# Five blocks of up to 512 tokens in both feed forwards of a sparse-attention and two-feed-forward kernel, with a new order of all the work around them

## The chip, the cores and the metric

The kernel runs on one core of a Trainium2 chip. Its time is the device time of one execution in microseconds (us), the median over several runs. A profile of one execution shows five engines that work in parallel, each in the order of its own queue: PE (TensorE: matmuls, with PEld for its weight loads), DVE (VectorE), ACT (ScalarE), POOL (GpSimd) and SP, which here only issues transfers.

## What is computed

Cut to what matters (4 sequences of 576 tokens, 8 heads of 64, so 2304 tokens of 512):

```python
# heads 0-3: local mask, 0 <= i - j < 32; heads 4-7: strided mask, i >= j and i % 32 == j % 32
scores = where(mask, q @ k.T / sqrt(64), -1e9)
x = softmax(scores) @ v                     # 2304 x 512, all heads side by side
h = x @ w_in                                # 512 x 2048, first feed forward ("moe")
x = (h * cos(h)) @ w_out                    # 2048 x 512
h = x @ w_in2                               # second feed forward ("moe2")
P = a0 + a1*h + a2*h**2 + a3*h**3
Q = 1 + |b0|*|h| + |b1|*h**2
out = (P / (Q + 1e-6)) @ w_out2
```

The weights arrive as 64-bit words of float64 (read as pairs of int32) and are decoded on the chip. Each fp32 product of the feed forwards is made of three matmuls: high part times high part, high times low, low times high.

## The kernel before

**Attention** is done in 32 items: `n` is a half sequence of 288 tokens (0 to 7), `pr` one of four pairs of heads. An item is scores (`att_s`, PE), maximum and subtraction or a softmax with a bias (DVE, POOL, ACT), exponentials (ACT), row sums and their reciprocals (DVE), the scaling (`att_norm`, POOL), transposes (`att_t`, PE) and their copies (`att_te`, ACT), the product with v (`att_o`, PE), and the split of the result into a high part `xh` (ACT) and a low part `xl` (DVE) in `att_oe`.

**A feed forward** goes over blocks of tokens, and in each block over 16 slices `f` of the 2048 inner columns. One block and one `f` is a step `g`. A step has 12 matmuls of the first layer (`l1`, line 415) into a bank `h`, elementwise work on `h`, and 12 (first feed forward) or 3 for every 128 tokens (second) matmuls of the second layer (`l2`, line 434), which are issued `LAG` steps later. In the first feed forward the elementwise work is called by letters: U (phase as an integer, ACT; `u` on DVE), K (a copy of `h`, ACT), V (fraction, DVE), N (sine, ACT), M (times `h`, DVE), G (high part `gh`, ACT), H (low part `gl`, POOL; `h` on DVE). Before, the blocks of the first feed forward have 256, 256, 352 and five times 288 tokens, the two of 256 sharing one set of four banks `y`; the second has six blocks of 384.

**Weights** of the first feed forward (32 tiles of 128 x 512) are decoded while the first steps run: two ACT instructions per tile (`dec_abs`), two on DVE (`dec_ops`, lines 156 and 158), then a high part on ACT and a low part on POOL or DVE (`w_split`). Those of the second are decoded later with three DVE instructions per tile, written to memory and read back.

**What sets the order.** Nothing is reordered by a scheduler: instructions are issued as the program writes them (`manual_schedule`). Before step 0 stands the list `START` of hand-written commands; from step 0 on, the string `ORD[g]` (or `C_ORD`) gives the order of a step's letters on ACT, DVE and POOL, and tables of step numbers (`TAB1`, `TAB2`, `TABE`, `TABO`, `W2ABS`, `DSTEP`) say in which step attention items, loads and decodes go. Before, `START` holds the whole of half `n` = 0 and the scores of half `n` = 1; the transposes and products of `n` = 1 come in steps 0 to 6. PSUM has eight banks: two `a`, two `h`, four `y`.

Of the kernel before, what the change touches and what calls it, by code (L numbers as in the profile page):

```python
# [8 lines left out]
F32 = mybir.dt.float32  # L9
# [10 lines left out]
NT = B * S  # L20
# [14 lines left out]
NB2 = 384  # L35
LAG = 3
LAG_AB = 2
RING = 3 * HS
HALF_COL = [0, HS, 2 * HS, 0, HS, 0, HS, 0]
NEG = -1e30  # L40
ABUFS = 4
BLAG = 7
NWARM = 38
NKEEP = 25
W2TAB = [(-7, -4, -3, -2, -1), (0, 3, 4, 4, 4), (4, 7, 8, 8, 9)]
TAB = ((-4, -2, -1, 0, 6, 9, 11), (-3, -1, 0, 1, 6, 10, 12), (0, 12, 2, 3, 6, 11, 13), (1, 13, 4, 5, 6, 12, 14))
# [12 lines left out]
ORD = {}
for _g in (0, 1, 23):  # L60
    ORD[_g] = "ukjVTswxyzNMabpqGHL"
COPY = {ord(c): None for c in "Kk"}
NPRE = 4
EVB, STB = 4, 6
LATE_OE = False
DSTEP = [0, 1, 2, 3, 4, 5, 6, 8, 10, 12, 14, 16]
# [11 lines left out]
W2ABS = [[25, 28, 29, 30, 31], [34, 37, 38, 38, 38], [37, 40, 41, 41, 42], [41, 44, 45, 45, 46], [48, 51, 52, 52, 52], [52, 55, 56, 56, 57], [57, 60, 61, 62, 63], [64, 67, 68, 68, 68], [68, 71, 72, 72, 73], [73, 76, 77, 78, 79], [80, 83, 84, 84, 84], [84, 87, 88, 88, 89], [89, 92, 93, 94, 95], [96, 99, 100, 100, 100], [100, 103, 104, 104, 105], [105, 108, 109, 110, 111]]  # L80
BLAG = 8
START = ['cst ACT', 'lq 0 0', 'lq 0 2 ACT', 'load 2 0', 'lv 0 1', 'lv 0 3 w0', 'lq 0 3', 'lq 0 1 ACT', 'load 0 0', 'lv 0 0', 'load 0 1', 'load 1 0 ACT', 'load 1 1', 'warm 38', 'lv 0 2 w0', 'masks', 's 0 0 y', 's 0 1 y', 's 0 2 y', 's 0 3 y', 'lq 1 0', 'ab', 'lq 1 2', 'lq 1 1', 'load 2 1', 'load 3 0', 'load 3 1', 'red 0 0', 'lv 1 0', 'exps 0 0', 'lq 1 3', 'ms 0 1', 'ex 0 1', 'red 0 2', 'lv 1 1', 'exps 0 2', 'norm 0 0 POOL', 'ms 0 3', 'ex 0 3', 'load 4 1', 'sum 0 1', 'norm 0 2 POOL', 'norm 0 1 POOL', 'sum 0 3', 'warm 29', 'abs 0 0', 'abs 0 1', 't 0 0 h', 'load 4 0', 'te 0 0', 'd 0 0 0', 'norm 0 3 POOL', 'o 0 0', 'd 0 1 0', 'd 0 0 1', 'd 0 1 1', 'd 0 0 2', 'd 0 1 2', 't 0 1 y', 'abs 1 1', 'te 0 1', 'oe 0 0', 'split 0 1 POOL', 'abs 1 0', 't 0 2 h', 'o 0 1', 'd 1 1 0', 'd 1 1 1', 'd 1 0 0', 'te 0 2', 'load 6 1', 'd 1 0 1', 'split 0 0 POOL', 'd 1 0 2', 't 0 3 y', 'oe 0 1', 's 1 0 y', 'te 0 3', 'd 1 1 2', 'o 0 2', 'split 1 0 POOL', 'oe 0 2', 'split 1 1 POOL', 'o 0 3', 's 1 1 y', 'abs 2 0', 'abs 2 1', 'd 2 0 0', 'd 2 1 0', 'abs 3 0', 'd 2 0 1', 'd 2 1 1', 'abs 3 1', 's 1 2 y', 's 1 3 a', 'red 1 0', 'd 2 1 2', 'red 1 1', 'd 2 0 2', 'exps 1 0', 'oe 0 3', 'split 2 0 POOL', 'exps 1 1', 'red 1 2', 'split 2 1 POOL', 'd 3 1 0', 'red 1 3', 'exps 1 2', 'exps 1 3', 'd 3 0 0', 'd 3 0 1', 'd 3 1 1', 'd 3 0 2', 'd 3 1 2', 'split 3 0 POOL', 'load 5 0', 'load 5 1', 'load 7 0', 'split 3 1 POOL DVE', 'load 7 1', 'load 6 0', 'next']
LV1 = [2, 4]
TABE = [[-5, -2, -1, 0, 4, 9, 11], [-3, -1, 0, 1, 6, 10, 12], [0, 12, 2, 3, 6, 11, 13], [1, 13, 4, 5, 6, 12, 14]]
TABO = [[-4, -2, -1, 0, 4, 9, 11], [-3, -1, 0, 1, 6, 10, 12], [-2, 12, 2, 3, 4, 11, 13], [1, 13, 4, 5, 6, 12, 14]]
C_ORD.update({0: 'swNMUKjVGHTL', 1: 'swNMUjVGhTL', 2: 'swNMUKjVGhTL', 3: 'swNMUKjVGhTL', 4: 'swNMUKjVGhTL', 5: 'swNMUKjVGhTL', 6: 'swNMUKjVGhTL', 7: 'swNMUkjVGHTL', 8: 'swNMUKjVGHTL', 9: 'swNMUKjVGHTL', 10: 'swNMUKJVGhTL', 11: 'swNMUKjVGhTL', 12: 'swNMUKjVGhTL', 13: 'swNMUKjVGhTL', 14: 'swNMUKjVGHTL', 15: 'swNMUKjVGHTL', 16: 'swNMUKjVGHTL', 17: 'swNMUKjVGhTL', 18: 'swNMUKjVGhTL', 19: 'swNMUKjVGhTL', 20: 'swNMUKjVGHTL', 21: 'swNMUKjVGhTL', 22: 'swNMUKjVGhTL', 23: 'swNMUjVGhTL', 24: 'swNLMUKjVGHT', 25: 'wNsMUKjVGHTL', 26: 'swNMUKjVGhTL', 27: 'swNMUKjVGhTL', 28: 'swNMUKjVGhTL', 29: 'swNMUKjVGhTL', 30: 'swNMUKjVGHTL', 31: 'swNMUKjVGHTL'})
W2RD = [4, 6, 2]
X2RD = [4, 2, 2]


@with_exitstack
def attention_moe_moe_kernel(ctx: ExitStack, tc: tile.TileContext, qk0, qk, vv, w1, w2, consts, a, b, out):
# [840 lines left out]
```

## Time and profile before

| | |
|---|---|
| timed runs | median 956.54 us of 3 (956.15 to 957.25) |
| span of the profiled execution, first to last instruction | 952.7 us |
| PE busy | 910.9 us of it (96%) |
| DVE, ACT, POOL busy | 692.0, 700.4, 292.7 us |

The span is that of one profiled execution; the 3.8 us by which the median is longer lie around it. Busy time counts overlapping instructions of an engine once. Matmuls are pipelined: a matmul's duration is longer than its distance to the next one, so the distances between starts are what counts for PE.

### The profile page before, as it was taken

The numbers are of one execution on the slowest core, as the hardware profiler recorded it, in microseconds if no ns is written. First come the engines' busy times: TensorE is split into PE (matmuls) and PEld (weight loads), VectorE is DVE, ScalarE is ACT, GpSimd is POOL, SyncE is SP. The second block draws the span as 40 slices with busy tenths as digits, with TensorE's granted clock in tenths as the row PEclk, the third lists the DMA queues.
The fourth block names the chain that finished last, engine by engine and source line by source line (L and its number), as shares of the span: only waits on it lengthen the run. The fifth ranks groups of instructions, "written<-read, shape, count | busy, mean of one in ns | idle before, by whom it ended". The sixth has DMA issues, their size and how long they took to land.

```text
span 952.7 us, 17284 instructions
## 1 busy us (share of the span) xinstructions
PE 910.9 (96%) x6367; PEld 859.7 (90%) x6367; DVE 692.0 (73%) x1330; ACT 700.4 (74%) x1454; POOL 292.7 (31%) x279
## 2 busy tenths in 40 slices
PE   7678999999999999999999999999999999999998
PEld 6567999999999989999999989999999999999996
DVE  4888755687565675666767798777777777777776
ACT  5987765665565764866757898788787788788875
POOL 2577732132222132122222224223233232232221
PEclk9799999999999999999999999999999999999999
DMA  9766102624334444244316620020020100200000
GB/s 317 270 223 217 46 1 78 209 67 130 120 133 151 139 130 154 74 133 161 130 61 186 194 81 1 1 67 1 1 67 1 40 28 1 67 1 1 34 1 34
DMA packets 51525, 89.35 MB, mean 94 GB/s; under 512 B 4584, under 2 KB 28400, under 8 KB 51440
## 3 DMA queue, kind: packets, MB, share of 16 engines
q1 hardware_dynamic: 50720, 86.58, 27.5%
q10 hardware_dynamic: 720, 1.67, 0.5%
q8 instruction: 50, 0.82, 0.4%
q14 instruction: 35, 0.29, 0.1%
HBM read 70.40 MB, written 17.83 MB: 93 GB/s over the span
## 4 chain that ended last, share of the span: by engine, by line
PE 78%; DVE 8%; ACT 8%; issue 3%; DMA 2%; POOL 1%; SPq 0%; ACTq 0%; DVEq 0%; POOLq 0%
PE y L434 35%; PE h L415 27%; PE a L415 10%; DVE dec L158 2%; PE a L250 2%; PE a L370 2%; DVE t L520 1%; PE a L351 1%; ACT dec L144 1%; DVE dec L611 1%; DMA v<-in_vv_dram 1%; ACT u L518 1%; ACT L518 1%; ACT t L506 1%; ACT L283 1%
## 5 line engine op out<-in xcount | busy, mean ns | idle before, releaser
L415 PE MATMUL h<-xh,w 128*128 128x288 f32 (+3 forms) x1408 | 338.6, 312 | 12.6 <-DVE t L520 10.4
L415 PEld LDWEIGHTS h<-xh,w 128*128 128x128 f32 x1408 | 245.3, 191 | 18.0 <-DVE t L520 11.6
L434 PE MATMUL y<-gh,w 128*128 128x288 f32 (+2 forms) x1024 | 229.2, 300 | 0.6 <-ACT w L164 0.6
L415 PE MATMUL h<-xl,w 128*128 128x288 f32 (+3 forms) x704 | 206.9, 310 | 0.0
L434 PE MATMUL y<-w,gh 128*128 128x512 f32 x576 | 193.2, 390 | 0.9 <-ACT ev L450 0.9
L476 POOL TENSOR_TENSOR z<-q,r 128x384 f32<-128x384 f32 x96 | 97.7, 1018 | 280.4 <-ACT r L475 277.0
L434 PEld LDWEIGHTS y<-gh,w 128*128 128x128 f32 x1024 | 172.1, 189 | 0.8 <-ACT w L164 0.8
L434 PE MATMUL y<-gl,w 128*128 128x288 f32 (+2 forms) x512 | 151.5, 296 | 2.2 <-POOL gl L526 2.1
L415 PEld LDWEIGHTS h<-xl,w 128*128 128x128 f32 x704 | 134.7, 191 | 1.8
L434 PEld LDWEIGHTS y<-w,gh 128*128 128x128 f32 x576 | 108.1, 188 | 21.1 <-ACT ev L450 1.2
L526 POOL TENSOR_TENSOR gl<-t,gh 128x288 fp32r<-128x288 f32 (+2 forms) x67 | 67.2, 1004 | 183.4 <-ACT gh L524 157.4
L506 ACT ACTIVATE t<-h,biases 128x288 int32<-128x288 f32 (+2 forms) x116 | 57.8, 498 | 88.6 <-PE h L415 77.5
L516 DVE SCALAR_TENSOR_TENSOR u<-h,t 128x288 f32<-128x288 f32 (+2 forms) x128 | 58.3, 455 | 77.0 <-ACT hs L512 60.7
L434 PE MATMUL y<-w,gl 128*128 128x512 f32 x288 | 112.7, 391 | 0.2 <-DVE gl L490 0.2
L465 DVE SCALAR_TENSOR_TENSOR q<-q,z 128x384 f32<-128x384 f32 x96 | 53.9, 562 | 78.8 <-ACT z L463 78.8
L415 PE MATMUL a<-xh,w 128*128 128x384 f32 x384 | 106.2, 337 | 0.0
L434 PEld LDWEIGHTS y<-gl,w 128*128 128x128 f32 x512 | 97.1, 190 | 3.0 <-POOL gl L526 2.9
L524 ACT ACTIVATE gh<-t 128x288 fp32r<-128x288 f32 (+2 forms) x128 | 56.9, 445 | 29.3 <-DVE t L520 27.4
L518 ACT ACTIVATE u<-u,biases 128x288 f32<-128x288 f32 (+2 forms) x128 | 68.0, 531 | 12.7 <-DVE u L516 12.4
L415 PEld LDWEIGHTS a<-xh,w 128*128 128x128 f32 x384 | 70.5, 188 | 1.8
L520 DVE TENSOR_TENSOR t<-u,hs 128x288 f32<-128x288 f32 (+1 forms) x91 | 50.5, 555 | 25.7 <-ACT u L518 25.0
L415 PE MATMUL a<-xl,w 128*128 128x384 f32 x192 | 64.9, 338 | 0.0
(117 smaller groups left out, 1593.5 us busy)
## 6 DMA issues: line engine op xcount, KB each, us to landing
raw<-in_w_dram SPq DMA_DIRECT2D x63, 512.0 KB
qk<-in_qk_dram SPq DMA_DIRECT2D x18, 481.0 KB
wf<-dec SPq DMA_DIRECT2D x32, 256.0 KB
wf<-wf SPq DMA_DIRECT2D x32, 256.0 KB
x2s<-x2d SPq DMA_DIRECT2D x24, 192.0 KB
out_dram<-ev SPq DMA_DIRECT2D x17, 256.0 KB
v<-in_vv_dram SPq DMA_DIRECT2D x16, 240.0 KB
v<-in_vv_dram SPq DMA_DIRECT2D x24, 157.5 KB
```

Of the source, the lines that this page charges most:

```text
L158: DVE.scalar_tensor_tensor(out=mi, in0=t[:, :, 1], scalar=-0x80000000, in1=mi, op0=ALU.bitwise_and, op1=ALU.bitwise_or)
L250: PE.matmul(sv[:, i], qb, rhs, start=not mask, stop=not mask or i == nb - 1 and mx is None)
L415: PE.matmul(h[:, :n], w[d["ph"], f, 0][:, 128 * c:128 * c + 128], x[c][:, cs], start=k == 0, stop=k == len(ops) - 1)
L434: PE.matmul(y, l, r, start=first and i == 0 and bk != bB, stop=last and i == 2 and bk != bA)
L465: DVE.scalar_tensor_tensor(out=q, in0=q, scalar=1.0 + 1e-6, in1=z, op0=ALU.add, op1=ALU.add)
L476: POOL.tensor_tensor(out=z, in0=q, in1=r, op=ALU.mult)
L506: ACT.activation(out=k, in_=h, func=AF.Identity, scale=INV_2PI, bias=biases[:, 2:3])
L516: DVE.scalar_tensor_tensor(out=u, in0=h, scalar=INV_2PI, in1=k, op0=ALU.mult, op1=ALU.subtract)
L518: ACT.activation(out=u, in_=u, func=AF.Sin, scale=TWO_PI, bias=biases[:, 3:4])
L520: DVE.tensor_tensor(out=t, in0=u, in1=e.get("hs", h), op=ALU.mult)
L524: ACT.activation(out=e["gh"], in_=t, func=AF.Copy)
L526: (POOL if c == "H" else DVE).tensor_tensor(out=e["gl"], in0=t, in1=e["gh"].bitcast(F32), op=ALU.subtract)
```

## The change

The tokens of both feed forwards are cut anew: 512, 352, 480, 480, 480 in the first, 384, 512, 512, 512, 384 in the second. The ring of columns `xh`, `xl` grows from 864 to 1152, and a half sequence may lie in it in pieces (`PIECES`); a block's results go to memory in runs (`PH1`). There are 160 steps in place of 224. All eight attention items of the first sequence (`n` = 0 and 1) now stand in `START`, ahead of step 0, with the decode of two pairs of weight tiles; the other 14 pairs are decoded one in a step, in steps 0 to 13. Scores of all items are made as two 64 x 64 matmuls for each block of queries, where those from `n` = 2 on were one 128-row matmul with zeros between. The copy K is gone: M reads `h` from its bank, and `u` and `t` are one tile. `l2` comes two steps behind in the first feed forward (before two, from the third block on three) and three in the second. Each attention item from `n` = 2 on has its own row of eight steps (`PAIR`), each weight tile of the second feed forward its own row (`W2T`), and the order of every step is written anew.

```diff
-NB2 = 384
-LAG = 3
-LAG_AB = 2
-RING = 3 * HS
+NA, NC, ND, NW = 512, 352, 480, 512
+LAG, LAG2 = 2, 3
+RING = 1152
+PH1 = [(NA, 0, [(0, 0, NA)]), (NC, 512, [(0, 512, NC)]), (ND, 0, [(0, 864, ND)]),
+       (ND, 672, [(0, 1728, 96), (96, 1440, 288), (384, 1344, 96)]), (ND, 192, [(0, 2016, 288), (288, 1824, 192)])]
+PH2 = [(384, 768), (512, 0), (512, 640), (512, 0), (384, 768)]
-NPRE = 4
+NPRE = 2
...
+PAIR = {-4: (1, 1, 2, 3, 5, 6, 8, 9),
...
-            for i in range(nb):
...
-                if n < 2:
-                    for j in range(2):
...
-                qb = t[:, 128 * (i0 + i):128 * (i0 + i) + 128]
-                PE.matmul(sv[:, i], qb, rhs, start=not mask, stop=not mask or i == nb - 1 and mx is None)
+                for j in range(2):
+                    r = slice(D * j, D * j + D)
+                    q0 = D * (i0 + i) if kc == QC else 128 * (i0 + i) + D * j
+                    PE.matmul(sv[r, i], t[r, q0:q0 + D], rhs[r], start=not mask, stop=not mask or i == nb - 1)
...
-bA, bB = block(1, 256, 0, 0), block(1, 256, 256, 256)
...
-bC = block(1, 3 * HS - 512, 512, 512)
+for n, xcol, runs in PH1:
+    blocks.append(dict(ph=1, n=n, xcol=xcol, runs=runs, y=None))
+    steps += [(len(blocks) - 1, f) for f in range(NF)]
...
-        elif c in "Kk":
-            e["hs"] = ep.tile([128, NB2], F32, tag="hs", name="hs")[:, :t.shape[1]]
...
         elif c == "M":
-            DVE.tensor_tensor(out=t, in0=u, in1=e.get("hs", h), op=ALU.mult)
+            DVE.tensor_tensor(out=u, in0=u, in1=h, op=ALU.mult)
...
-    for k in range(NPRE, NF):
-        dplan[DSTEP[k - NPRE]] = pairs[k]
+    dplan = {k - NPRE: pairs[k] for k in range(NPRE, NF)}
```

PE, where step 0 begins. Before, its first matmul (line 415) follows the scores of half `n` = 1 (lines 239 and 247), whose transposes come later:

```order
L239 MATMUL y<-cst_78 128x252
L247 MATMUL y<-k_226,qk 64x126 x4
L239 LDWEIGHTS cst_78
L239 MATMUL a<-cst_78 128x378
L247 MATMUL a<-k_250,qk 64x126 x6
L239 LDWEIGHTS cst_78
L239 MATMUL a<-cst_78 128x252
L247 MATMUL a<-k_250,qk 64x126 x4
L415 MATMUL h<-xh_85,w_404 128x256
L415 MATMUL h<-xl_89,w_404 128x256
```

Now its first matmul (line 478) follows the last products of that half (line 443) and their transposes (line 421):

```order
L421 MATMUL y<-cst,p 126x128 x5
L443 MATMUL y<-pt_573,v 64x63 x6
L443 MATMUL y<-pt_575,v 64x63 x2
L443 MATMUL y<-pt_575,v 64x36 x2
L443 MATMUL h<-pt_599,v 64x63 x6
L443 MATMUL h<-pt_601,v 64x63 x2
L443 MATMUL h<-pt_601,v 64x36 x2
L478 MATMUL h<-xh_83,w_632 128x512
L478 MATMUL h<-xl_87,w_632 128x512
L478 MATMUL h<-xh_84,w_632 128x512
```

Four transposes and four products have moved from behind step 0 to ahead of it, and the matmuls are of 512 columns.

DVE, two early steps. Before (line 516 is V, 520 is M, 156 and 158 the two decodes; low parts of weights are on POOL here):

```order
L516 SCALAR_TENSOR_TENSOR u<-h,t 128x256
L156 SCALAR_TENSOR_TENSOR dec<-dec,raw 128x512 x2
L520 TENSOR_TENSOR t<-u,h 128x256
L158 SCALAR_TENSOR_TENSOR dec<-raw,dec 128x512 x2
L516 SCALAR_TENSOR_TENSOR u<-h,t 128x256
L156 SCALAR_TENSOR_TENSOR dec<-dec,raw 128x512 x2
L520 TENSOR_TENSOR t<-u,h 128x256
L158 SCALAR_TENSOR_TENSOR dec<-raw,dec 128x512 x2
```

Now, one early step and the start of the next (563 is V, 567 is M, 248 and 250 the decodes, 263 the low part of a weight tile, 572 the low part `gl`):

```order
L563 SCALAR_TENSOR_TENSOR u<-h,u 128x512
L263 TENSOR_TENSOR w_709<-dec,w_709 128x512
L248 SCALAR_TENSOR_TENSOR dec<-dec,raw 128x512 x2
L567 TENSOR_TENSOR u<-u,h 128x512
L263 TENSOR_TENSOR w_716<-dec,w_716 128x512
L250 SCALAR_TENSOR_TENSOR dec<-raw,dec 128x512 x2
L572 TENSOR_TENSOR gl<-u,gh 128x512
L263 TENSOR_TENSOR w_762<-dec,w_762 128x512
L248 SCALAR_TENSOR_TENSOR dec<-dec,raw 128x512
L563 SCALAR_TENSOR_TENSOR u<-h,u 128x512
```

A step still has the decode of two tiles, but V and M cover 512 columns, and some low parts, of weights and of `g`, stand on DVE. In the first 16 steps POOL keeps 14 of the 28 low parts of weights and 10 of the 16 `gl`.

PE, scores in a running step. Before and now:

```order
L415 MATMUL h<-xh_88,w_450 128x256
L250 MATMUL a<-qk 128x89 x5
L434 MATMUL y<-gh,w_657 128x256
```

```order
L478 MATMUL h<-xh_86,w_642 128x512
L335 MATMUL a<-qk 64x89 x10
L495 MATMUL y<-gh,w_645 128x512
```

The five matmuls of an item's scores have become ten of half the rows and half the columns of the array, at the same place, between `l1` and `l2`.

## Rows read from the trace of the kernel before

**Rows 1.** The page: span and busy time by engine.

```profile
span 952.7 us, 17284 instructions
PE 910.9 (96%) x6367; PEld 859.7 (90%) x6367; DVE 692.0 (73%) x1330; ACT 700.4 (74%) x1454; POOL 292.7 (31%) x279
```

**Rows 2.** Windows by stage; columns as in the first line, PEclk the granted clock.

```profile
core 0: us, PE busy (x) PEld busy (x) DVE busy (x) ACT busy (x) POOL busy (x), PEclk, DMA share, GB/s
0.00:35.29 35.29, 25.06 (x340) 20.70 (x340) 20.90 (x48) 24.94 (x77) 11.25 (x13) 0.90 0.99 326
35.29:97.25 61.96, 45.62 (x367) 42.93 (x365) 53.89 (x75) 52.15 (x121) 44.60 (x35) 0.86 0.61 209
97.25:542.80 445.55, 435.22 (x3615) 427.35 (x3613) 299.22 (x612) 295.05 (x636) 118.05 (x115) 1.00 0.37 121
542.80:952.74 409.94, 405.04 (x2054) 368.73 (x2052) 317.95 (x596) 328.23 (x623) 118.78 (x118) 1.00 0.08 27
```

**Rows 3.** Waits of PE between 35.29 and 97.25: total, times, longest.

```profile
PE h L415 <- DVE t L520: 6.6, 2, 4.8
```

**Rows 4.** Timeline of PE: first matmul of two steps each, of 256, 352, 288 columns.

```profile
97.25 0.28 PE L415 MATMUL h<-xh,w 128*128 128x256 f32 x1
100.10 0.28 PE L415 MATMUL h<-xh,w 128*128 128x256 f32 x1
...
186.97 0.32 PE L415 MATMUL h<-xh,w 128*128 128x352 f32 x1
190.82 0.33 PE L415 MATMUL h<-xh,w 128*128 128x352 f32 x1
...
498.56 0.29 PE L415 MATMUL h<-xh,w 128*128 128x288 f32 x1
501.73 0.29 PE L415 MATMUL h<-xh,w 128*128 128x288 f32 x1
```

**Rows 5.** Chain that ended last, a step of the second feed forward: start, us.

```profile
559.37 2.10 PE h L415 x12
561.47 2.05 PE y L434 x9
```

**Rows 6.** Timeline of PE: scores of an item packed (x20), and later unpacked (x10).

```profile
6.53 0.98 PE L247 MATMUL y<-qk 64*64 64x89 f32 x20
7.45 0.21 PE L236 MATMUL y<-msk,cst 128*128 128x89 bf16 x1
104.53 1.24 PE L250 MATMUL a<-qk 128*128 128x89 f32 x10
105.56 0.36 PE L434 MATMUL y<-gh,w 128*128 128x256 f32 x1
```

**Rows 7.** Windows of 6.24 to 35.29; and of PE's line 351 (transposes) after 35.29.

```profile
6.24:35.29 29.05, 20.39 (x302) 16.24 (x302) 20.28 (x42) 23.66 (x76) 11.05 (x9) 0.88 1.05 345
35.29:97.25 61.96, 3.90 (x20) 2.81 (x20) 0.86 0.61 209
```

**Rows 8.** The same of PE's line 370 (products with v).

```profile
35.29:97.25 61.96, 3.67 (x80) 3.14 (x80) 0.86 0.61 209
```

**Rows 9.** Groups by line and shape: DVE's V, M and low part; POOL's low part.

```profile
L516 DVE SCALAR_TENSOR_TENSOR u<-h,t 128x256 f32<-128x256 f32 x32 | 13.4, 420 | 8.6 <-ACT t L506 8.3
L516 DVE SCALAR_TENSOR_TENSOR u<-h,t 128x352 f32<-128x352 f32 x16 | 8.4, 523 | 12.1 <-ACT hs L512 8.4 <-ACT t L506 3.6
L167 DVE TENSOR_TENSOR w<-wf,w 128x512 fp32r<-128x512 f32 x32 | 22.6, 741 | 3.4 <-ACT w L164 3.1
L167 POOL TENSOR_TENSOR w<-dec,w 128x512 fp32r<-128x512 f32 x32 | 45.6, 1437 | 24.5 <-ACT w L164 24.0
```

**Rows 10.** Timeline: two decodes on DVE, POOL idle at the first, busy at the second.

```profile
37.02 1.28 DVE L156 SCALAR_TENSOR_TENSOR dec<-dec,raw 128x512 int32<-128x512 int32 x2
47.06 2.38 DVE L156 SCALAR_TENSOR_TENSOR dec<-dec,raw 128x512 int32<-128x512 int32 x2
47.29 1.61 POOL L167 TENSOR_TENSOR w<-dec,w 128x512 fp32r<-128x512 f32 x1
```

More of the change, by code (lines that the diff above doesn't have):

```diff
@@ L137, in w_load, with dec_abs @@
         raws[key, f, o] = t
-    def dec_abs(key, f, o, eng=None, low=True):
+    def dec_abs(key, f, o, eng=None):
         t = raws.pop((key, f, o))
+        low = key == 1 and (f, o) not in M3
         m = stage("dec")
@@ L433, in l2 @@
             for i, (l, r) in enumerate(ops):
-                PE.matmul(y, l, r, start=first and i == 0 and bk != bB, stop=last and i == 2 and bk != bA)
+                PE.matmul(y, l, r, start=first and i == 0, stop=last and i == 2)
     def evac(bk):
         d = blocks[bk]
-        n, t0 = d["n"], 0 if bk == bB else d["tok"]
+        n = d["n"] if d["ph"] == 1 else 512
+        end = bk == len(blocks) - 1
         for c, y in enumerate(d["y"]):
             t = stage("ev")
-            if d["ph"] == 2 or bk == bB:
-                n = 512
             src = y[:, :n]
-            if bk == len(blocks) - 1 and c == len(d["y"]) - 1:
+            if end and c == len(d["y"]) - 1:
                 ACT.activation(out=t[:, :256], in_=src[:, :256], func=AF.Copy)
@@ L451, in evac @@
             if d["ph"] == 1:
[L452 to L454 removed]
+                for c0, t0, m in d["runs"]:
+                    SP.dma_start(out=x2d[:, c, t0:t0 + m], in_=t[:, c0:c0 + m])
+            else:
+                t0 = d["tok"] + 128 * c
+                (ACT if end and c == len(d["y"]) - 1 else SP).dma_start(out=out[t0:t0 + 128, :], in_=t)
     def ew_a(p, bk, h):
         n = blocks[bk]["n"]
[L460 to L461 removed]
+        t = ep.tile([128, NW], F32, tag="u", name="t")[:, :n]
+        q, z, r = (p.tile([128, NW], F32, tag=k, name=k)[:, :n] for k in "qzr")
         ACT.activation(out=q, in_=h, func=AF.Square, scale=root[:, 0:1])
@@ new lines, in plan_attention @@
+        for k, (lq, lv, ss, ms, xs, us, ts, os) in PAIR.items():
+            n, i = divmod(k + 12, NP)
+            if lq is not None:
+                plan("load", lq, att_lq, p, n, i)
+            if lv is not None:
+                plan("load", lv, att_lv, p, n, i)
+            plan("pe", os, att_o, n, i)
+            plan("pe", ss, att_s, n, i)
+            plan("pe", ts, att_t, n, i)
+            plan("E", ts, att_te, p, n, i, DVE if k in TED else None)
+            plan("O", os, att_oe, n, i)
+            plan("1", ms, att_max, p, n, i, POOL)
+            plan("2", xs, att_exp, n, i)
+            plan("3", us, att_sum, p, n, i)
+            plan("3", us, att_rec, n, i)
+            plan("4", us, att_norm, n, i, POOL)
@@ new lines, in plan_attention, with first, nth, third @@
+        for kind in ("pe",):
+            for key in [x for x in plans if x[0] == kind]:
+                plans[key].sort(key=lambda x: [att_o, att_s, att_t].index(x[0]))
+    def plan_w2(p):
+        for j, (ld, g0, g1, g2, g3) in enumerate(W2T):
+            f, o = divmod(j, 2)
+            plan("load", ld, w_load, p, w2, 2, f, o)
+            def first(f=f, o=o):
+                raws["m", f, o] = dec_abs(2, f, o)
+            def nth(c, f=f, o=o):
+                dec_ops(c, *raws["m", f, o])
+            def third(f=f, o=o):
+                r = raws.pop(("m", f, o))
+                dec_ops(4, *r)
+                SP.dma_start(out=wf[f, o], in_=r[1])
+            plan("d", g0, first)
+            plan("e", g1, nth, 3)
+            plan("f", g2, nth, 2)
+            plan("i", g3, third)
```

522 lines of the change are left out of this document (237 added, 285 removed), and 33 rows, old and new, of tables (PAIR, START, W2T).

## The prediction

> **What bounds the kernel now.** I read the page first: PE is busy 96% of the span, DVE 73%, ACT 74%, POOL 31% [rows 1]. Then I cut the span into four stages at step boundaries [rows 2]. From 97.25 on PE has its full clock (1.00) and is busy 98 to 99%; DVE and ACT are at 67 to 80%. There, only less work on PE makes the kernel shorter. The first 97.25 us are another kernel. Up to 35.29 PE makes no matmul of the feed forward; attention of half 0 and the first weights come through ACT (24.94 of 35.29 busy), DVE and transfers (DMA share 0.99). From 35.29 to 97.25 twelve steps of 256 columns run while weights are decoded: DVE is busy 53.89 and ACT 52.15 of 61.96, PE only 45.62, at a mean clock of 0.86. The longest wait there, 4.8 us, is of `l1` for M on DVE [rows 3].
>
> A matmul's price on PE is the distance between step starts. A step of 24 matmuls takes 2.85 us at 256 columns, 3.85 at 352, 3.17 at 288 [rows 4]: 119, 160 and 132 ns each. In the second feed forward 12 matmuls of 384 take 2.10 us and 9 of 512 take 2.05 [rows 5]: 175 and 228 ns. So a matmul costs about 0.41 ns a column and 13 to 18 ns on top, and fewer, longer matmuls are cheaper by the part on top.
>
> The profiled execution's span is 952.74 us; the median of the runs is 956.54, so 3.80 lie around the span, and I carry that over.
>
> **The sum, part by part.**
>
> *First feed forward on PE.* At 512 columns the row gives 228 ns, 24 make 5.47 us; at 480, on the line from 175 (384) to 228 (512), 214.6 ns, 5.15 us; 352 stays at 3.85. Sixteen steps each: 87.5 + 61.6 + 3 x 82.4 = 396.3 us. Before: 32 x 2.85 + 16 x 3.85 + 80 x 3.17 = 406.4. This is 10.1 us less.
>
> *Second feed forward.* Stage 4 has 96 steps of 4.15, 398.4, and 11.5 us more at its two ends. After: 32 x 4.15 + 48 x 5.47 = 395.4, and the same ends, since the last block again has 384 columns and `l2` is again three steps behind: 406.9 in place of 409.94.
>
> Together 1344 matmuls fall away. The Trainium skill, TensorE: Matmul & The Clock Gate, section "Wait — 56ns, not 53.3ns?", gives a warm matmul's distance as its columns at 2.4 GHz and about 2.5 ns. By that the 1344 are worth 3.4 us and not 13, and the time would be 940. The trace disagrees: 228 ns for 512 columns [rows 5] is about 14.5 over 213.3.
>
> *Attention in the loop.* Stage 3 has 20 steps of 256, 16 of 352 and 80 of 288: 57.0 + 61.6 + 253.6 = 372.2. The other 73.4 of its 445.55 are the 24 items of n = 2 to 7: 3.06 each. They stay. Their scores: ten packed matmuls take 0.92 us from start to start at 89 columns (records are doubled: x20), five unpacked 1.03 [rows 6]. Twelve items gain 0.11; those of other widths I take as even. This is 1 us, bounds 0 and 3 either way.
>
> *The start.* Four more items go through transposes, products, copies and splits before step 0. PE: in 6.24 to 35.29 it was busy 20.39 us [rows 7], and the four items' transposes and products, 3.90 and 3.67 in the next stage, come ahead [rows 7, 8]: 28.0. Without a wait step 0 would begin at 34.2; at the same use, 20.39 of 29.05, at 46.1. ACT sheds eight instructions of decodes and high parts, since half the tiles are wanted by then, and gains twelve shorter ones (two exponentials, six copies, four splits): at most 3 us on its 23.66, and by ACT alone, used as before, step 0 would begin at 39 at the latest. I take 43 for step 0's start, nearer to PE's upper bound, since PE waits for each item's chain through four engines; bounds 34 and 47. The weights' transfers are issued before they are wanted and I cost them at nothing; the cover is the softmax work, and without it one tile late costs what it is late, as every decode behind it on ACT waits too.
>
> *The decode over 16 steps.* PE's own demand is 5.47 and some 5.5 items at 3.06 over 16 steps, 1.06: 6.53 us a step. DVE's in the 14 steps with a decode: V on the line from 420 (256) and 523 (352) is 0.69 at 512 [rows 9], M, the same kind, 0.67; four decode instructions at 0.64 with POOL idle (1.28 for two [rows 10]) 2.56; one low part of a weight 0.74 [rows 9]; six `gl` in 16 steps 0.28; a third of an item, about 1.0. Together 5.94, below PE. With POOL busy two decodes take 2.38 [rows 10]: 1.19 each, and DVE needs 8.14, above PE. POOL's list in these steps: 14 weights and 10 `gl` at 1.44, 12 attention instructions at about 1.0, some 46.6 us, 45% of the time. At 45% DVE needs 6.93, 0.40 over PE in 14 steps: 5.6 us. Filling the pipe comes on top: step 2's `l1` must wait for M of step 0, since `h` has two banks, and everything on PE stands behind it, `l2` of step 0 too; with the clock not yet up, 2.4 us. I take 8 us in all; bounds 0 (PE alone) and 26 (all of it with POOL busy: 14 x 1.61 + 3).
>
> *New waits in the loop.* Without K, bank `h` is held until M is done. Between the end of one `l1` and the next into the same bank stand `l2`, `l1`, `l2`: 7.7 us at 480 columns, 5.8 at 352. The chain U, V, N, M is four instructions of about 0.65, 2.6 us, and one item's exponentials between at most doubles it. It fits; I cost it at nothing, and ACT is relieved of a copy each step. A new block's first `l2` needs its bank `y` emptied, as before.
>
> Sum: 43 + 396.3 + 73.4 - 1 + 8 + 406.9 = 926.6; with 3.8 around it **930 us**, 2.8% below 956.54. Checked against before: 35.29 + 61.96 + 445.55 + 409.94 is the span, and stage 2 had 61.96 - 12 x 2.85 = 27.8 us over its steps, of which 7.6 were the four items; the other 20.2 were waits and low clock, for which I now allow 8.
>
> **Rivals.**
> *Decode is bound by DVE and POOL.* DVE's operations on two SBUF tiles and POOL's take turns whenever both have work [rows 10], DVE needs 8.14 a step, and the 8 us become 26: 948. For it: DVE is at 87% in stage 2 with POOL at 72% [rows 2]. Against: low parts moved from POOL to DVE cut POOL's share to 45%. The Trainium skill, SBUF — State Buffer, section "SBUF: two separate sides", says that the two engines' shared port is locked for a whole instruction and the other blocks fully; by that all of POOL's 46.6 us could be added to DVE's list. The rows agree for a pair of decodes (1.28 and 2.38).
> *The start is a chain.* If the items' chains follow each other rather than interleave, step 0 begins at about 55, PE used at 28.0 of 49, and the time is 942. For it: PE's use between 6.24 and 35.29 was 70% with half the chains. Against: a list that alternates items.
> *Longer matmuls save nothing.* If a matmul cost 0.458 ns for each column whatever its length (288 columns), 512 would be 234 ns: the time is 930 + 13 = 943. Against it: the row of 512 [rows 5].
> *Slower: bank `h` binds every step of the first feed forward.* M reads `h`, and where it is late `l1`, and behind it all of PE, waits, as in the 4.8 us of stage 2 [rows 3]. It decides once 80 steps lose 0.33 us each, 26.5 us together. At 0.5 us a step the time is 970. Against: 7.7 us of room for a chain of 2.6 to 5.
>
> **How the numbers follow.** My forecast has 0.65, its own range 921 to 942. Decode bound 0.17 (948), start a chain 0.06 (942), columns alone 0.03 (943), bank `h` 0.09 (from 948 to 980, two thirds of it above 956.54). The lower end is the start at 34 (-9) and no wait in the decode (-8), of which I take most: 916; the upper end takes in decode at its bound and part of a late start, 952. A difference under 0.2%, 1.9 us, is about what a measurement of this kernel cannot tell from none. Faster by more: 0.91; within: 0.03; slower: 0.06.
>
> **What the profile after would show.** The first `l1` at 41 to 46 us; step 16 about 112 us later; DVE at 90% and POOL near 45% in between. From then on PE at 98%, steps of 5.47, 5.15 and 3.85 us where no attention stands in them. The second feed forward 407 us. A wait list of PE with `l1` on DVE's M at more than 20 us in total would make the bank rival right; PE idle and DVE full until step 14 the decode rival. I would be wrong on the large side if DVE or ACT, not PE, filled the steps after 16.

## The result, and the profile after

The changed kernel takes 922.77 us (median of 4 runs, 920.53 to 923.93), the kernel before 956.89 beside it: ratio 0.9643, 95% interval 0.9628 to 0.9657. Forecast were 930 us and a range of 916 to 952. The page is to be read against [rows 1], and the windows by stage against [rows 2]. The cuts are the first matmuls of step 0, of step 16 (first of 352 columns) and of the second feed forward:

```profile
span 921.6 us, 14207 instructions
PE 891.8 (97%) x5263; PEld 760.9 (83%) x5263; DVE 661.9 (72%) x1162; ACT 624.5 (68%) x1106; POOL 239.1 (26%) x203
```

```profile
0.00:43.11 43.11, 29.87 (x439) 25.03 (x439) 24.23 (x64) 23.75 (x78) 6.15 (x10) 0.92 1.00 296
43.11:150.46 107.35, 101.19 (x601) 80.43 (x602) 93.83 (x155) 91.33 (x157) 45.14 (x34) 0.95 0.43 145
150.46:513.85 363.39, 358.85 (x2378) 313.90 (x2376) 233.35 (x441) 198.42 (x351) 72.47 (x63) 1.00 0.42 131
513.85:921.62 407.77, 401.92 (x1849) 341.55 (x1847) 310.47 (x506) 310.96 (x524) 115.33 (x97) 1.00 0.09 30
```

The span fell by 31.1 us: PE is busy 19.1 us less and idle 12.0 us less (952.7 - 910.9 = 41.8 before, 29.8 now). The second feed forward gave 2.2 us (409.94 to 407.77), everything ahead of it 28.9 (542.80 to 513.85).

What a matmul costs now, from the chain that ended last (start, us; 12 matmuls of 512 columns each) and from PE's timeline (the last `l1` of 480 columns, then the first of the second feed forward; and an attention item's products, L443, and scores, L335, between `l1` and `l2`):

```profile
640.61 2.72 PE a L478 x12
643.33 2.72 PE y L495 x12
```

```profile
508.65 0.37 PE L478 MATMUL h<-xh,w 128*128 128x480 f32 x1
...
513.85 0.33 PE L478 MATMUL h<-xh,w 128*128 128x384 f32 x1
...
170.57 0.80 PE L443 MATMUL a<-pt,v 89*64 89x58 f32 x20
171.30 0.98 PE L335 MATMUL a<-qk 64*64 64x89 f32 x20
172.21 0.43 PE L495 MATMUL y<-gh,w 128*128 128x352 f32 x1
...
108.08 0.71 PE L421 MATMUL a<-cst,p 128*89 128x128 f32 x5
108.55 0.49 PE L495 MATMUL y<-gh,w 128*128 128x512 f32 x1
```

A step of 512 takes 5.44 us, one of 480 5.20. Of an item, the products take 0.73 us from start to start, the scores 0.91 at 89 columns (1.03 in [rows 6]), the transposes 0.47: 2.1 us together. PE's waits over the whole span (total, times, longest):

```profile
PE h L443 <- DMA v<-in_vv_dram: 6.1, 1, 6.1
PE a L335 <- DVE p L360: 4.0, 5, 1.2
PE h L478 <- ACT w L260: 2.6, 1, 2.6
PE a L421 <- DVE xl L457: 2.1, 1, 2.1
PE a L421 <- POOL p L412: 1.7, 2, 1.3
PE h L478 <- DVE u L567: 1.6, 2, 0.9
```

The wait of [rows 3] (`l1` for M, here L567) was 6.6 us between 35.29 and 97.25 alone; now it is 1.6 over the whole span. The longest is new: at the end of the start PE waits 6.1 us for v of one item, and then 2.6 us for a weight tile on ACT. Waits of 2.6 us (for L567, L412 and L360) and of 2.1 us (for L457) belong to two steps that stand out, 8 and 12, with about 10 us each, where step 10 with transposes of the same kind takes 6.05. Windows of steps 8, 10 and 12:

```profile
88.28:98.23 9.95, 8.19 (x29) 6.20 (x30) 9.78 (x17) 8.61 (x17) 6.95 (x5) 0.83 0.00 0
105.36:111.41 6.05, 6.05 (x31) 5.02 (x29) 5.30 (x9) 5.29 (x11) 1.02 (x1) 1.00 0.00 1
118.72:128.85 10.13, 8.05 (x30) 6.14 (x29) 7.71 (x13) 8.39 (x17) 5.08 (x5) 0.83 0.40 153
```

The granted clock of steps 8 and 12 is 0.83: full until the wait, and the lower of its two levels for a part of the `l2` behind it. As the experiments show, that is this execution's, and not this code's in every execution.

### The profile page after: what moved, and what is told of

It reads as the page before. It is cut to its first block, busy times and chain, and to the rows that moved or that the text cites. A ratio compares the mean times of both kernels' runs of the same rounds, so it can differ in the third digit from the quotient of the medians.

```text
span 921.6 us, 14207 instructions
## 1 busy us (share of the span) xinstructions
PE 891.8 (97%) x5263; PEld 760.9 (83%) x5263; DVE 661.9 (72%) x1162; ACT 624.5 (68%) x1106; POOL 239.1 (26%) x203
## 4 chain that ended last, share of the span: by engine, by line
PE 81%; DMA 7%; ACT 6%; DVE 4%; issue 1%; SPq 0%; ACTq 0%; POOL 0%; DVEq 0%
PE y L495 39%; PE h L478 27%; PE a L478 10%; DMA raw<-in_w_dram 3%; PE a L335 2%; DMA v<-in_vv_dram 2%; PE a L443 2%; PE a L421 1%; DMA qk<-in_qk_dram 1%; DMA ab<-in_a_dram 1%; ACT dec L233 1%; DVE w L263 1%; ACT w L260 1%; ACT gh L570 1%; ACT raw L238 1%
## 5 line engine op out<-in xcount | busy, mean ns | idle before, releaser
L478 PE MATMUL h<-xh,w 128*128 128x480 f32 (+3 forms) x960 | 296.6, 370 | 4.2 <-ACT w L260 2.6
L495 PE MATMUL y<-gh,w 128*128 128x480 f32 (+2 forms) x640 | 205.0, 382 | 0.0
L478 PEld LDWEIGHTS h<-xh,w 128*128 128x128 f32 x960 | 178.9, 188 | 30.0 <-DVE u L567 2.9
L478 PE MATMUL h<-xl,w 128*128 128x480 f32 (+3 forms) x480 | 178.5, 372 | 0.0
L537 POOL TENSOR_TENSOR z<-q,r 128x512 f32<-128x512 f32 (+1 forms) x80 | 94.7, 1184 | 279.8 <-ACT r L536 276.9
L495 PE MATMUL y<-gl,w 128*128 128x480 f32 (+2 forms) x320 | 119.9, 375 | 0.2 <-DVE gl L572 0.2
L478 PE MATMUL a<-xh,w 128*128 128x512 f32 (+1 forms) x320 | 98.2, 367 | 0.0
L565 ACT ACTIVATE u<-u,biases 128x480 f32<-128x480 f32 (+2 forms) x80 | 54.4, 680 | 61.3 <-DVE u L563 60.3
L495 PEld LDWEIGHTS y<-w,gl 128*128 128x128 f32 x288 | 54.1, 188 | 12.7 <-DVE gl L550 2.2
L478 PE MATMUL a<-xl,w 128*128 128x512 f32 (+1 forms) x160 | 59.1, 369 | 0.0
```

The lines of the kernel that those rows point to most:

```text
L478: PE.matmul(h[:, :n], w[d["ph"], f, 0][:, 128 * c:128 * c + 128], x[c][:, cs], start=k == 0, stop=k == len(ops) - 1)
L495: PE.matmul(y, l, r, start=first and i == 0, stop=last and i == 2)
L537: POOL.tensor_tensor(out=z, in0=q, in1=r, op=ALU.mult)
L565: ACT.activation(out=u, in_=u, func=AF.Sin, scale=TWO_PI, bias=biases[:, 3:4])
```

## Experiments

My theory: outside the start PE is the bound, a matmul costs its columns and a part on top, and what PE loses it loses where one thing comes late. The main rival: DVE and POOL, not PE, bound the steps with a decode. Ratios are to the kernel before, as above.

**The late v transfer (v_earlier).** `START`, SP's commands:

```diff
- 'lv 1 1 w0', 'load 2 0', ..., 'load 3 0', 'load 1 0', ..., 'lv 1 3 w0',
+ 'lv 1 1 w0', 'lv 1 3 w0', 'load 2 0', ..., 'load 3 0', 'load 1 0', ...,
```

> The transfer of v for the last item of half 1 is issued ahead of three weight tiles, not behind them. Theory (this one transfer, for which PE waited 6.1 us, sets the end of the start): the last products at 33 to 34 in place of 39.3, step 0 at 37 to 38.5 in place of 43.1, the time 917 to 919. Rival (the transfers as a whole bound the start, their share is 1.00): the weight tiles come later by as much, PE waits for one of them instead, step 0 stays at 42 to 43 and the time at 922 to 923. Second rival (the decode catches up with it): step 0 is early, but steps 0 to 5 are longer by the same 5 us; 921 to 923.

918.6 us, ratio 0.9618 (0.9605 to 0.9631). Step 0 begins at 39.71, 3.4 us earlier, not 5 to 6 (in the nine traces with `START` unchanged it begins at 42.34 to 44.86). The v wait is gone; now `l1` waits 5.4 us for the high part of its weight. ACT's waits from 30 us on say why:

```profile
ACT dec L233 <- DMA raw<-in_w_dram: 2.3, 1, 2.3
```

The high part of step 0's tile stands on ACT behind the decode of another tile, and that one's transfer lands 2.3 us late. Theory and first rival hold in part: the v transfer set the start, and the next one sets it 3.4 us earlier.

**The queue behind one v (lv0_later).** In the changed kernel SP issues (start, length, count):

```profile
101.89 13.50 SPq L302 DMA_DIRECT2D v<-in_vv_dram  x2
...
115.49 1.86 SPq L224 DMA_DIRECT2D raw<-in_w_dram  x4
```

The second v waits for its buffer until the products two items before are done; four weight tiles stand behind it.

```diff
- 0: (8, 10, 11, 11, 14, 15, 16, 18),
+ 0: (8, 12, 11, 11, 14, 15, 16, 18),
```

> The v transfer of one later item is asked for two steps later. In the changed kernel it stood in SP's queue 13.5 us for its buffer, with four weight tiles behind it, one of which came 1.6 us late for its decode on ACT, and with it the copies that PE's transposes of step 12 waited for (2.08 us). Theory: step 12 falls from 10.14 us to about 6.1, which is what step 10 takes with the same work, because the stretch of lower clock behind the wait goes with the wait; the time is 918 to 919.5. Rival: only the wait goes, step 12 takes 8.0, the time is 920.5 to 921. Second rival: DVE is what is late there, step 12 stays at 10 and the time at 922 to 923.

The tiles go out from 109.51, and step 12 takes 7.05 in place of 10.13, at clock 1.00. The time is 920.9, ratio 0.9639 (0.9625 to 0.9653), which can't be told from 0.9643. The step can't be put down to the edit either. The runs halves, ff2_384, ff1_288 and ff1_288_order (below) have the changed kernel's first 16 steps as they are, and their v waits in SP's queue for 13.5 us too. Yet their step 12 takes 6.99 to 7.11 us, with a wait of 0.53 to 0.64. The queue, PE and step 12 in halves, then PE in the changed kernel:

```profile
101.63 13.49 SPq L302 DMA_DIRECT2D v<-in_vv_dram  x2
...
122.75 0.43 PE L421 MATMUL a<-cst,p 128*63 128x128 f32 x2 [0.56 <-DVE xl L457]
...
118.98:126.03 7.05, 6.49 (x31) 4.97 (x29) 6.47 (x10) 5.80 (x12) 3.47 (x3) 1.00 0.52 200
```

```profile
124.01 0.43 PE L421 MATMUL a<-cst,p 128*63 128x128 f32 x2 [2.08 <-DVE xl L457]
```

So most of the 2.08 us of wait, and the low clock behind it, are of the one execution that was profiled, and why it had them stays open. What goes with the edit is less: steps 11 to 15 take 36.6 us here and 37.7 to 38.0 in those four, so it is worth 1.0 to 1.4 us. My theory, that the late tiles made step 12 late, is not shown.

**More room for the sums (sum_first).**

```diff
- 6: 'yuVWskzN1ME2pqabGOH34',
+ 6: 'yuV34skN1MWzE2pqabGOH',
```

> In step 6 the row sums and the scaling of an attention item come ahead of two weights' pieces on DVE, so that the transposes of step 8 find it done. Theory: step 8 falls from 9.95 us to 6.1 to 6.8, the clock's loss going with the wait; the time is 919 to 920. Rival (DVE is full through these steps, 9.78 of 9.95 us busy): what is put ahead makes M late, the first matmul of step 8 waits for it longer than the 0.85 us of now, step 8 stays above 9 and the time is 922 to 924.

925.36, ratio 0.9684 (0.9671 to 0.9697): slower. Step 8 takes 13.81. Its transposes need two banks `a`. The scaling came in time, but the second bank was held by another item's scores until DVE took their maximum (L360), now behind W (a low part of a weight) and z (a piece of a decode). PE's and DVE's timelines:

```profile
91.95 0.49 PE L421 MATMUL a<-cst,p 128*89 128x128 f32 x3
96.97 0.70 PE L421 MATMUL a<-cst,p 128*89 128x128 f32 x2 [4.54 <-DVE p L360]
```

```profile
95.28 1.15 DVE L263 TENSOR_TENSOR w<-dec,w 128x512 fp32r<-128x512 f32 x1
96.36 0.47 DVE L360 TENSOR_TENSOR p<-a,cst 128x315 f32<-128x315 f32 x1
```

Of the 13.81 us, 4.54 are this wait; the granted clock of the step is 0.75. On DVE it was not only the order: what was moved now ran beside POOL. The first piece of z, here and then in the changed kernel:

```profile
89.63 1.52 DVE L252 TENSOR_SCALAR dec<-dec 128x512 int32<-128x512 int32 x1
```

```profile
86.48 0.41 DVE L252 TENSOR_SCALAR dec<-dec 128x512 int32<-128x512 int32 x1
```

POOL splits a weight tile from 89.12 to 90.86 in the first, and has done so by 86.01 in the second. The run is slower, as the rival said, and above its 922 to 924, by another way than it said: M was not late, but the maximum was.

**All three (all_three).**

> The three edits of the runs v_earlier, lv0_later and sum_first together. Theory (three separate late arrivals, each worth 3 to 5 us): they add to 11 to 13 us, step 0 at 37 to 38.5, steps 8 and 12 at 6 to 7, the time 910 to 912. Rival (the decode on ACT and DVE is close behind PE everywhere, and what is won in one place is waited for in the next): step 0 early, but steps 0 to 15 together not under 107, the time 916 to 920.

920.08, ratio 0.9632 (0.9618 to 0.9645). Step 0 begins at 40.15; step 12 takes 6.88 us, step 8 13.10. This is at the upper end of the rival's 916 to 920, but not for its reason: one of the three edits was a loss, and takes back most of what the other two gave.

**The part on top of a matmul (halves).** In the last block of the first feed forward:

```diff
...
+        if bk == 4:
+            for c0 in (0, 240):
+                xs = slice(d["xcol"] + c0, d["xcol"] + c0 + 240)
+                for k, (w, x, c) in enumerate(ops):
+                    PE.matmul(h[:, c0:c0 + 240], ..., x[c][:, xs], ...)
```

> In the last block of the first feed forward each first-layer matmul of 480 columns is made as two of 240: 192 matmuls more over 16 steps, the same columns. Theory (a matmul costs its columns and some 13 to 18 ns on top): a step without attention goes from 5.20 us to 5.36 to 5.42, the time up by 2.5 to 3.5 us, to 925 to 926.5. Rival (columns alone count): 5.20 as now and 923. Rival by the Trainium skill, TensorE: Matmul & The Clock Gate, section Wait — 56ns, not 53.3ns?, with 2.5 ns on top: 5.23.

```profile
482.10 0.27 PE L484 MATMUL h<-xh,w 128*128 128x240 f32 x1
...
484.79 0.38 PE L501 MATMUL y<-gh,w 128*128 128x480 f32 x1
...
487.39 0.27 PE L484 MATMUL h<-xh,w 128*128 128x240 f32 x1
```

24 matmuls of 240 take 2.69 us, 12 of 480 take 2.60: a step is 5.29, and a matmul more costs 8 ns. The time, 921.96 (ratio 0.9649, 0.9627 to 0.9671), can't tell 16 x 0.09 = 1.4 us. My 13 to 18 ns are not met, nor is "columns alone". By these two lengths a matmul has 7.5 ns of its own and each column 0.436, so over half of the 17 ns by which 480 columns exceed 200 (2.4 GHz) grows with the columns. The 2.5 ns of the Trainium skill (TensorE: Matmul & The Clock Gate, section "Wait — 56ns, not 53.3ns?") would, by an estimate, have made the step 5.23; the trace has 5.29.

**The second feed forward as before (ff2_384).**

```diff
-PH2 = [(384, 768), (512, 0), (512, 640), (512, 0), (384, 768)]
+PH2 = [(384, 768), (384, 0), (384, 384), (384, 768), (384, 0), (384, 384)]
```

> The second feed forward is cut into six blocks of 384 again, as before the change; the first stays. Theory (192 matmuls more, each with its part on top): 96 steps of 4.15 to 4.19 in place of 32 of 4.19 and 48 of 5.44, so 3 to 7 us more for this stage, 411 to 415, and 926 to 930 in all. Rival (columns alone count, or the elementwise chain hides it): the stage stays at 408, the time at 922 to 923.5.

928.06, ratio 0.9712 (0.9693 to 0.9732): slower than with 512 by some 5 us (6.6 by the ratios). A step of 384 (first and second layer):

```profile
738.10 0.33 PE L478 MATMUL h<-xh,w 128*128 128x384 f32 x1
...
740.21 0.39 PE L495 MATMUL y<-w,gh 128*128 128x512 f32 x1
...
742.29 0.33 PE L478 MATMUL a<-xh,w 128*128 128x384 f32 x1
```

It takes 4.19 us. 96 of them are 402, where 32 of 4.19 and 48 of 5.44 are 395. Before the change the same step took 4.15 [rows 5]; why 9 matmuls take 2.08 here and 2.05 there no run shows, and it is over half of the difference (96 x 0.04 = 3.8).

**The first feed forward with blocks of 288 (ff1_288, ff1_288_order).**

```diff
-(ND, 0, ...), (ND, 672, ...), (ND, 192, ...)]
+(288, 0, ...), (288, 864, ...), (288, 288, ...), (288, 576, ...), (288, 0, ...)]
...
+        if not late and g >= 32:
+            g = 32 + (g - 32) * 5 // 3
```

> The last three blocks of the first feed forward (480 tokens each) become five of 288, as before the change, with the tables of attention and of the second feed forward's weights stretched by 5/3 from step 32 on; the second feed forward stays. Theory (only PE counts there, and the matmuls' part on top): 80 steps of 3.17 in place of 48 of 5.20, 4 us more, the time 926 to 928. Rival (short steps don't cover the elementwise chain and the decode beside them, PE waits): 8 us and more, above 930. Rival (columns alone): 923.

1081.29, ratio 1.1316 (1.1294 to 1.1338). (The tokens' places in the ring change with the blocks.) From step 80 to 111, where no table has an order of its own and `C_ORD` holds, steps take 5 to 10 us. Waits of PE there, and the window:

```profile
PE y L495 <- ACT gh L570: 42.2, 30, 1.4
PE y L495 <- POOL gl L572: 25.7, 30, 3.1
```

```profile
444.55:674.50 229.95, 159.22 (x769) 144.80 (x768) 48.64 (x96) 54.53 (x125) 29.20 (x35) 0.78 0.12 39
```

No engine but PE is half busy. `l2` follows two steps behind, 3.17 us after the first layer whose end releases U, V, N and, behind them, the step before's G and H. So PE waits in nearly every step, and its clock has a mean of 0.78. The second run therefore changes the order alone, from step 32 on:

```diff
-C_ORD = "MdkEUVN1Gef23rOHi4"
+C_ORD = "MGkUhVEN1def23rOi4"
...
-        return ORD[g] if g in ORD else AB_ORD if g < NF else C_ORD
+        return ORD[g] if g < 2 * NF else C_ORD
```

> ff1_288 with another order of the elementwise work from step 32 on: M, high and low part of the step before (all on ACT and DVE) come ahead of this step's U, V and N, where they stood behind them. Theory (in ff1_288 a chain of some 3.2 us, from the end of a first layer to the low part that was queued behind it, met 3.17 us of room, since the second layer follows two steps behind; it is not PE's work or the decode that filled it): the waits on gh and gl go, 80 steps of 3.17 and the attention, 926 to 935. Rival (short steps don't cover the decode and attention on ACT and DVE at all): above 960 still.

960.49, ratio 1.0044 (1.0028 to 1.0061): 121 us less by an order, and still no faster than the kernel before. Most steps from 80 on take 3.16; but the block stage (233.83 to 548.17) takes 36 us more than with 480, of which the matmuls are 3.2 (80 x 3.16 less 48 x 5.20). PE's waits, whole span:

```profile
PE h L478 <- DVE u L567: 17.0, 18, 2.7
PE y L495 <- ACT ev L510: 9.0, 4, 5.6
```

That is my rival of bank `h`, at 288 columns: with 480 it lost 1.6 us. My expectation of 926 to 935 failed. The tables were stretched and the one order written without tuning, so 36 us is no fair price of 288, and no run shows what a tuned order would take. What is shown is that with two banks `h`, no copy, two steps of lag and these orders, the short steps leave waits that the long ones, with theirs, do not.

**DVE against POOL (low_pool, low_dve).** In steps 0 to 15 alone, the letters of the low parts:

```diff
+        return s.translate(str.maketrans('SWh', 'swH')) if g < NF else s
```

and for low_dve the other way, `('swH', 'SWh')`.

> In steps 0 to 15 all low parts, of weights and of g, go to POOL: DVE loses 20 instructions of 0.68, 14 us, POOL gains 20 of about 1.45 and is at about 70% there. Theory (DVE's operations on two SBUF tiles stretch while POOL works: in the changed kernel the decodes took 0.68 with POOL idle and 0.87 to 0.93 beside it, 9.6 us of excess over 46.9 us of POOL's work): DVE wins 14 and loses some 6 back, POOL's gl come later than DVE's and hold up the second layer; steps 0 to 15 together 105 to 109, the time 921 to 925. Rival (DVE's fill is all that makes steps 8 and 12 late, and POOL has room): they fall to about 7 each, the time 916 to 918. Rival (POOL becomes the bound as in the kernel before): above 928.

> In steps 0 to 15 all low parts, of weights and of g, go to DVE, the opposite of low_pool: 24 instructions of 0.68 more on DVE, 16.4 us, and POOL keeps 10 attention instructions. Theory (the two hinder each other, so that most of DVE's 9.6 us of excess goes with POOL's work): DVE's list grows by 8 to 10, to 102 of 107 us, PE waits more in steps 6 to 13, the time 925 to 930. Rival (no such hindrance, all 16 come on top): 932 and above. Rival (POOL's instructions, twice as long as DVE's, were what came late): 917 to 921.

low_pool 933.24 (ratio 0.9765, 0.9743 to 0.9786), low_dve 927.85 (0.9704, 0.9683 to 0.9726): both slower. Steps 0 to 15 take 115.37 and 111.76 us; the changed kernel has 107.35, and the four runs with its first 16 steps as they are 104.8 to 105.3. The two windows, low_pool first:

```profile
43.75:159.12 115.37, 102.56 (x601) 80.46 (x601) 97.85 (x135) 91.77 (x157) 75.66 (x54) 0.95 0.40 134
44.21:155.97 111.76, 101.10 (x601) 79.60 (x601) 99.16 (x177) 91.70 (x157) 12.09 (x11) 0.96 0.42 138
```

DVE's decodes in these steps, by group (count, busy us, mean ns), first of the changed kernel, then low_pool, then low_dve:

```profile
L248 DVE SCALAR_TENSOR_TENSOR dec<-dec,raw 128x512 int32<-128x512 int32 x27 | 21.6, 811 | 0.0
L250 DVE SCALAR_TENSOR_TENSOR dec<-raw,dec 128x512 int32<-128x512 int32 x30 | 21.4, 744 | 0.0
```

```profile
L248 DVE SCALAR_TENSOR_TENSOR dec<-dec,raw 128x512 int32<-128x512 int32 x27 | 31.4, 1182 | 0.0
L250 DVE SCALAR_TENSOR_TENSOR dec<-raw,dec 128x512 int32<-128x512 int32 x30 | 29.9, 1027 | 0.0
```

```profile
L250 DVE SCALAR_TENSOR_TENSOR dec<-raw,dec 128x512 int32<-128x512 int32 x30 | 20.4, 711 | 0.0
L248 DVE SCALAR_TENSOR_TENSOR dec<-dec,raw 128x512 int32<-128x512 int32 x27 | 18.1, 682 | 0.0
```

The same instructions take 38.5 us where POOL is busy for 12, 43.0 where it is busy for 45, and 61.3 where it is busy for 76. low_pool takes 14 us of work from DVE, and DVE is 4 us busier (97.85 for 93.83). Steps 8 and 12 do fall, to 7.41 and 6.53, but steps 7 and 11 rise to 9.98 and 12.76. The time is that of the last rival, but POOL is busy in 66% of these steps, no bound by itself: the theory had the mechanism and a third of its size. For low_dve it had the time; DVE is busy 5.3 us more, where I had said 8 to 10.

**A faster version (start_and_lv0, start_lv0_step6).** v_earlier and lv0_later, and in `START`:

```diff
- 'oe 1 3', 'd 1 1 1', 'abs 1 0', 'load 4 0', 'd 1 0 1', 'oe 1 1', 'split 0 0 DVE',
+ 'oe 1 3', 'oe 1 1', 'split 0 0 DVE', 'd 1 1 1', 'abs 1 0', 'load 4 0', 'd 1 0 1',
```

> The edits of v_earlier and lv0_later, and in the list ahead of step 0 the high and low part of step 0's weight tile (with the split of the last attention item that it needs) come ahead of the decode of another tile, whose transfer ACT waited for 2.35 us in v_earlier, with step 0's tile queued behind it. Theory (an arrival that is late for one tile holds up another only by the order on ACT): step 0 at 36 to 36.8 in place of 39.7, step 12 at 7.05, the time 914 to 916. Rival (the start is bound by its transfers as a whole, share 0.97 to 1.00): steps 0 to 4 become longer by as much, step 5 begins at 66 to 67 as in v_earlier, the time 917 to 919.

914.79, ratio 0.9573 (0.9547 to 0.9598), under the interval of the changed kernel: 8 us off by the times, 6.7 by the ratios. Step 0 begins at 37.61, step 16 at 142.17 in place of 150.46. In the four runs with steps 0 to 15 as they are, step 16 begins at 147.6 to 148.8, and these steps take as long as here (104.56): so the gain is that of the start. Step 2 is 1.4 us longer (8.06), so the rival has that much. In the second version, besides:

```diff
- -2: (4, 10, 5, 7, ...
+ -2: (4, 10, 5, 6, ...
...
- 6: 'yuVWskzN1ME2pqabGOH34',
+ 6: 'yuVWskzNME2341pqabGOH',
```

> start_and_lv0, and in step 6 the sums of one item and the maximum of the next one (moved up a step) come after M and ahead of the two second pieces of the decode, where sum_first had put them ahead of M and left the maximum where it was. Theory (sum_first failed because the maximum, which frees the second bank of the transposes, came 3.4 us later, not because DVE has no room): step 8 falls from 8.4 to 6.6 to 7.2, 1 to 1.8 us off the time of start_and_lv0. Rival (DVE is full from step 6 to 9, every order there waits somewhere): the time of start_and_lv0 or above, step 8 or 9 longer by 1 to 4 us.

915.67, ratio 0.9573 (0.9553 to 0.9593): no difference. Step 8 falls to 8.23 from 9.96 (there at a clock of 0.83; at 1.00 it takes 8.34 to 8.39 in six other traces, so the fall can be the clock's alone). Steps 9 to 11 rise by 1.9 us together. The rival is right for this order, which only moves the wait; two orders of step 6 that gain nothing make it likely, and don't show, that from step 6 to 11 the decode binds.

## Why the prediction came out as it did

The forecast's case came true, 5.0 us of span below the sum (921.6 for 926.6). The terms, one by one.

*The start, 43.* Measured 43.11, and half of the hit is luck. I let PE's upper bound stand for a chain through four engines and costed the transfers at nothing. PE waited twice at the end: 6.1 us for the transfer of v, and 2.6 for step 0's weight tile, which stood on ACT behind another tile's decode. Moving commands alone brought step 0 to 37.61.

*First feed forward on PE, 396.3.* 16 x 5.44 + 16 x 3.85 + 48 x 5.20 = 398.2: the line to 480 was 0.05 us a step low. But the last two steps' `l2`, 5.2 us, fall behind the cut at 513.85, and there they are part of the 11.5 us of ends. I counted them twice; 393.0 belonged here.

*Attention, 73.4 less 1.* Three rows of an item add to 2.1 us, 24 items to 50.4. My 3.06 was what was left of stage 3 of before, with all its waits in it (PE idle for 445.55 - 435.22 = 10.3 us there). This term was 22 us too large.

*The decode and the waits, 8.* What is left of the 470.74 us between step 0 and the second feed forward is 470.74 - 393.0 - 50.4 = 27.3. In steps 0 to 15 it is 107.35 - 30 x 2.72 - 5.4 x 2.1 = 14.4 (14 `l2` and 16 `l1`, 5.4 items by their matmul records), and 12.9 behind. So these steps lost nearly twice what I took for them, 2.1 to 2.6 us of it only in this execution, as the four runs with the same steps show. This too is a remainder and no duration: PE is idle for 6.2 us of the 14.4 (107.35 - 101.19) and 4.5 of the 12.9 (363.39 - 358.85). The rest is lower clock (granted 0.61 in step 0, 0.83 in steps 8 and 12) and, behind step 16, where the clock is 1.00, matmuls and items that took longer in their place than the rows by which I priced them. The rival of DVE and POOL was right at most in a stretch, steps 6 to 11. It was not the 26 us that it was priced at, and the decodes' rows show why: POOL's 45 us left DVE most of its speed (43.0 us for the decodes, 38.5 beside 12 us of POOL).

*Second feed forward, 406.9.* Measured 407.77; 512 was 0.03 us a step cheaper, 384 0.04 dearer.

Together: 0.1 + (393.0 - 396.3) + (50.4 - 72.4) + (27.3 - 8) + 0.9 = -5.0. The step that failed is the price of an item: it was a remainder, not a duration, and its surplus of 22 us happened to pay for the 19 us of waits and low clock that I left out. The total was closer than its terms, by luck.

*Rivals.* Bank `h` lost 1.6 us in the first feed forward's 80 steps; the mechanism is real at 288 columns. Columns alone: the 1152 matmuls fewer of the first feed forward came to 8.2 us (406.4 to 398.2), not to the 10.1 that I gave them, 7 ns each, as in halves. Packed scores: 0.12 us an item at 89 columns, as said. The other widths are not even: 63 columns take 0.73 us, and 126 take 1.23 where nothing is waited for, against 1.03 unpacked:

```profile
158.37 1.30 PE L335 MATMUL a<-qk 64*64 64x126 f32 x20
159.60 0.50 PE L495 MATMUL y<-gh,w 128*128 128x512 f32 x1
```

Over 24 items that is 12 x 0.12 + 6 x 0.30 - 6 x 0.20 = 2.0 us. The other five items of 126 columns wait besides for DVE's maximum (L360) between their matmuls, 4.0 us together in the list above; this is the largest wait outside the start. Of the signs, step 0, the second feed forward, PE's steps of 512 and 480 columns (5.44 and 5.20) and its 98% held. Step 16 came 107 us behind step 0, not 112, and DVE was 87% busy there, POOL 42%.

*Where the 28.9 us ahead of the second feed forward came from.* Before, the same count gives 507.51 (stages 2 and 3) - 401.6 (406.4 less three `l2` of 1.58) - 24 x 2.23 - 4 x 1.20 (the transposes and products of four items, that are now in the start) = 47.6 us lost on PE between step 0 and the cut; now it is 27.3. So some 20 us are waits and low clock that went, 8 to 9 the matmuls, 2 to 3 the items' scores; the start took 8 us more, 5 of them matmuls that came out of stage 2. PE's idle time alone, by the windows, bears most of the 20 out: 16.3 and 10.3 us in stages 2 and 3 before, 6.2 and 4.5 now, 16.0 less. That the sharing of low parts between DVE and POOL is part of it is shown (low_pool gives 10 us of the time back, low_dve 5). That long steps cover what short ones don't is seen in ff1_288_order, with an order that nobody tuned. What the decode over 16 steps of 512 in place of 12 of 256 gave by itself stays open: no run took it back alone. So the larger part of the gain has its place shown, and its cause only in part.

## What to carry to other kernels

Price each piece by its own rows, start to start: a remainder of a stage holds that stage's waits, and a change that takes these away changes the price. A longer block may first buy cover (each queued chain gets more time under one step's matmuls) and only then fewer instructions: here some 20 us of waits and low clock went, and some 11 us of matmuls in both feed forwards. When a start is moved, walk the transfer queue too: two late arrivals, found in the waits of PE and then of ACT, were worth most of 7 to 8 us here for an edit of order. And before a step of one profiled execution is explained, look at the same step in the traces of other runs that leave it as it is: step 12 would have told me that 3 us of it were no property of the code.

## What the runs showed of the hardware

The same waits before the same matmuls did not always cost the same. Step 8 has idle pieces of about 0.86, 1.29 and 0.47 us in the changed kernel and in v_earlier, lv0_later, halves, ff2_384, ff1_288 and ff1_288_order. It takes 9.95 us at a granted clock of 0.83 in the first, and 8.34 to 8.39 at 1.00 in the six others. In lv0_later:

```profile
89.56:97.95 8.39, 6.63 (x29) 5.06 (x30) 8.29 (x15) 7.04 (x14) 5.44 (x4) 1.00 0.00 0
```

In the changed kernel the matmuls behind the wait are at the lower of the two levels for some 3 us. So the same 2.6 us of waits leave the step 2.3 us longer than step 10 (6.05) in six traces and 3.9 us longer in one, and a step's time of one execution tells the two apart only with its clock beside it. In start_and_lv0 the step has 1.8 us of waits and takes 9.96, again at 0.83: a shorter wait that cost more.

The slowing of DVE beside POOL grew faster than POOL's work: 4.5 us on 57 decodes from 12 to 45 us of POOL, 18.3 more from 45 to 76. In the same windows V, which reads `h` from PSUM, kept its 0.68 to 0.69 us.
